# Half of the filter matrix M loaded crosswise ahead of x and copied across by GpSimd, and the filter built by channel halves ahead of x's stage

## The chip, the cores and the metric

The kernel runs on one core of one Trainium2 chip. The metric is the device time of one execution in microseconds (us), given as the median of several runs. A core has a TensorE (PE; its weight loads are shown as PEld), a VectorE (DVE), a ScalarE (ACT), a GpSimd (POOL) and a SyncE (SP); POOL and SP issue the kernel's DMAs, each in the order of its own queue.

## The reference

```python
def _attn_ref(x, h):                      # x: 8 x 5696 x 128, h: 5696 x 128
    L = 2 * S                             # S = 5696, D = 128
    Xf = np.fft.rfft(x, n=L, axis=1)
    Hf = np.fft.rfft(h, n=L, axis=0)
    y = np.fft.irfft(Xf * Hf[None], n=L, axis=1)[:, :S, :]      # a long causal convolution

def _moe_ref(x, w_r, w_i, w_ch):          # x is y of the above, n_modes = 64
    X = np.fft.rfft(x, axis=1)
    # the lowest 64 modes are mixed over channels by a complex 128 x 128 matrix each
    Yr = einsum('bmd,mde->bme', Xr, w_r) - einsum('bmd,mde->bme', Xi, w_i)
    Yi = einsum('bmd,mde->bme', Xr, w_i) + einsum('bmd,mde->bme', Xi, w_r)
    u = x + irfft(Y)
    return u + relu(u @ w_ch)
```

Inputs and output are float32; the kernel works in float16 with float32 sums in PSUM.

## The kernel before

**Tiling.** A sequence of 5696 positions is cut into NQ = 89 rows of J = 64. A transform of length 11392 is taken in two steps: a step over the 89 rows (constant `f1_sb`, NK = 90 frequencies with real and imaginary part), and then a step over the 64 positions with twiddle factors, for each frequency k by its own 64 x 192 block of the constant M (`m_sb`, line 222): the columns are minus the imaginary part, the real part, the imaginary part. Two batches are taken together ("a pair"); there are four pairs.

**The prologue**, which the change rewrites, runs in this order.

- POOL issues h's load into `h_in` (two DMAs, float32 to float16), then the first pair's x in eight pieces of two DMAs each into `x_raw` (tile Xr), then M in six pieces (lines 386-388). M is stored twice in the constant, in partitions 0-63 and again in 64-127 shifted by 64 columns, so that both halves of the partitions hold all of it.
- DVE clears half of Hp and of Xin, and ACT the rest of Xin. PE runs `idle(57, 6)`, 57 matmuls on f1 that fill the time until h lands.
- DVE copies h into Hp in four parts (line 413). The **h stage** (lines 416-429) has 16 tiles of 16 matmuls (a 128 x 64 block of Hp as weights against 90 columns of f1); each tile's result of 128 x 720 is evacuated into Ah by ACT, or by DVE for every fourth one. Behind every second tile's evacuation DVE runs `x_place` (line 359), which copies one piece of x from Xr into Xin.
- **x's stage** (lines 672-677) has 32 tiles of `a_tile` (line 444): four matmuls with 128 x 128 of Xin as weights against 180 columns of f1, evacuated into As (128 x 720), by ACT or DVE as the function `share` decides from planned costs. Every `a_tile` needs all eight pieces of x in place. Between these tiles stand twelve `filter_couple`s (line 463): eight frequencies of the filter each, one 128 x 128 matmul per frequency of M against Ah, evacuated as 128 x 1024 into Hs. When a group of couples is complete, SP moves its two partition halves crosswise within Hs (tile Hs from Hs, ten DMAs).
- `idle(4)`, and then the **main stage**: for each pair 23 ticks of `second` (M against As), `products` (times the filter Hs), `third` and `modes_of`, and then the next pair's x stage of 32 `a_tile`s. After the last pair comes the output stage.

PSUM has eight banks; the x stage takes them two at a time in the order of `SLOTS = [0, 2, 4, 6]`. Each engine runs its own list in the order in which the program adds operations; a recorder (`Recorder`, line 21) puts a semaphore wait before an operation wherever its inputs or its room depend on another engine. So DVE's list, for instance, is in program order: a copy that waits holds up the evacuations behind it.

Other places that the text below speaks of: `clear_zt` (line 511), a POOL memset; `reflect` (line 518), a DVE `tensor_scalar` from SBUF to SBUF near the output stage.

Of the kernel before, what the change touches and what calls it, by code (L numbers as in the profile page):

```python
# [123 lines left out]
def bass_long_conv_fft__then__afno_spectral_mix_kernel(nc, x, h, moe_w_r, moe_w_i, moe_w_ch, out):  # L124
# [20 lines left out]
    strip = np.stack([-mat.imag, mat.real, mat.imag], axis=2).reshape(J, NK * 3 * J)  # L145
    MW = NK * 3 * J + J
    mt = np.zeros((P, MW))
    mt[0:J, 0:NK * 3 * J] = strip
    mt[J:P, J:MW] = strip
    th = 2.0 * np.pi * np.outer(pp, pp) / J  # L150
# [55 lines left out]
    def at(name, cols, dt, off):  # L206
        return nc.alloc_sbuf_tensor_at(name, [P, cols], dt, offset=off)
# [26 lines left out]
    DH = D // 2  # L234
    hp_sb = at("Hp", J * XS, F16, a_as)
    XC = 4
    XN = J // XC
    XB = XN * D
    x_raw = [at(f"Xr{i}", XB, F16, a_h + 2 * XB * i) for i in range(2 * XC)]
    x_st = [at(f"Xt{i}", XB, F16, a_as + i * XB * 2) for i in range(2 * XC)]  # L240
# [48 lines left out]
    def pv(bank, off, dims, p0=0, n=P):  # L289
        return bass.AP(ps, p0 * 4096 + bank * 512 + off, [[4096, n]] + [list(d) for d in dims])  # L290
# [5 lines left out]
    def bank(i):  # L296
        return ("bank", i)
# [18 lines left out]
    def dma(eng, dst, src, ring, reads=(), writes=(), after=()):  # L316
        R.add(eng, lambda h_: h_.dma_start(dst, src), reads, writes, ring=ring, after=after)  # L317

    def mm(o, l, r, st, sp, reads, writes):
        R.add("tensor", lambda h_: h_.matmul(o, l, r, start=st, stop=sp), reads, writes)  # L320
# [11 lines left out]
    def turns(name, items):  # L332
        i = ring2.get(name, 0)
        ring2[name] = i + 1
        return items[i % len(items)]
# [3 lines left out]
    dma("sync", f1_sb[:, :], c_f1.ap(), "c", (), [("f1",)])  # L339
    zr = [t_[J:P, 0:J * XS].bitcast(U32) for t_ in (hp_sb, x_sb)]  # L340
    R.add("vector", lambda e: e.memset(zr[0], 0), (), [("hz",)])
# [32 lines left out]
    wp = w_pieces()  # L374
    WD = [p_[3] for p_ in wp]
    for i in range(2 * XC):
        x_load(0, i, x_raw[i], [("xr", i, 0), ("xr", i, 1)])
    XZ = [("xz", 0), ("xz", 1)]
    XIN = [("xin", i) for i in range(2 * XC)]
    XR = [[("xr", i, p_) for p_ in range(2)] for i in range(2 * XC)]  # L380
    MP = 6
    GP = 2 * KT
    NS = NK // 2 + 1
    NG = (NS + GP - 1) // GP
    KP = NK // MP
    for i in range(MP):
        lo, hi = i * KP * 3 * J, (i + 1) * KP * 3 * J + (J if i == MP - 1 else 0)
        dma("gpsimd", m_sb[:, lo:hi], bass.AP(c_m, lo, [[MW, P], [1, hi - lo]]), "x", (), [("m", i)])
    dma("sync", sg_sb[:, :], c_sg.ap(), "c", (), [("sg",)])
    dma("sync", wc_sb[:, :], bass.AP(c_w, 0, [[3 * P, P], [1, 2 * P]]), "c", (), [("wc",)])  # L390

    def mtok(k):
        t = [("m", k // KP)]
        if k % KP == KP - 1 and k < NK - 1:
            t.append(("m", k // KP + 1))
        return t

# [13 lines left out]
    DC = D // 4  # L411
    for c_ in range(4):
        R.add("vector", lambda e, c_=c_: e.tensor_copy(
            bass.AP(hp_sb, c_ * DC, [[J * XS, NQ], [XS, J], [1, DC]]),
            bass.AP(h_in, c_ * DC, [[J * D, NQ], [D, J], [1, DC]])), HT, [("hp", c_)])
    for j in range(16):
        t = turns("h", [0, 2, 4])
        for i in range(8):
            d = 8 * j + i
            for r in range(2):  # L420
                mm(pv(t + i // 4, (i % 4) * NK, [[1, NK]], J * r, J), ap(hp_sb, J * XS, 0, P, d, [[XS, J]]),
                   ap(f1_sb, 2 * NK, 0, P, r, [[2, NK]]), True, True,
                   [("hz",), ("hp", d // DC), ("f1",)], [bank(t + i // 4)])
        evac(bass.AP(ah_sb, 8 * j, [[HW, P], [D, NK], [4, 2], [1, 4]]),
             pv(t, 0, [[1, NK], [512, 2], [NK, 4]]),
             [bank(t), bank(t + 1)], [("ah", j)], 1.0 / 64,
             eng="vector" if j % 4 == 1 else "scalar")
        if j % 2 == 0:
            x_place(j // 2, x_raw[j // 2], XR[j // 2])

    load = {"scalar": 0.0, "vector": 0.0}
    COST = {720: (670, 815), 1024: (910, 1130), 256: (280, 330)}

    def share(n):
        a, v = load["scalar"] + COST[n][0], load["vector"] + COST[n][1]
        e = "scalar" if a <= v else "vector"
        load[e] = min(a, v)
        return e

    HP = [("hz",)] + [("hp", c_) for c_ in range(4)]  # L440
# [22 lines left out]
    def filter_couple(c_, sl, eng):  # L463
        ks = [k for t in (2 * c_, 2 * c_ + 1) if t < NT for k in ticks[t]]
        n = len(ks)
        for i, k in enumerate(ks):
            mm(pv(sl + i // KT, i % KT * D, [[1, D]]), m_sb[:, k * 3 * J + J:k * 3 * J + 3 * J], ah_sb[:, k * D:k * D + D], True, True,
               AHT + mtok(k) + [("ag", k)], [bank(sl + i // KT)])
        lo, t1 = ks[0] * D, min(2 * c_ + 1, NT - 1)
        hi = lo + n * D  # L470
        old = once("xr", [t_ for r_ in XR for t_ in r_]) if c_ == 0 else []
        evac(h_sb[:, lo:hi], pv(sl, 0, [[1, n * D]]), [bank(sl), bank(sl + 1)], [("h", t, 0) for t in range(2 * c_, t1 + 1)],
             eng=eng, after=old)
        if t1 in HEND:
            g0 = ([-1] + HEND)[HEND.index(t1)] + 1
            lo = KT * g0 * D
            for p0, p1 in ((0, J), (J, 0)):
                dma("sync", h_sb[p0:p0 + J, HW + lo:HW + hi], h_sb[p1:p1 + J, lo:hi], "s", [("h", i, 0) for i in range(g0, t1 + 1)],
                    [("h", i, 1, p0) for i in range(g0, t1 + 1)])
# [8 lines left out]
    def load_w(i):  # L488
# [6 lines left out]
            [("zs", i, b) for i in range(NZ) for b in range(2)]  # L495
    M_ALL = [("m", i) for i in range(MP)]
    G_ALL = [("g", i) for i in range(NG)]
    WT = [("w", i) for i in range(NWP)]
    ZY = [("zs", i, b) for i in range(NZL, NZX) for b in range(2)]
    ZX = [("zs", i, b) for i in range(NZ, NZL) for b in range(2)]  # L500
    zt_old = [(AST, AST), (AST, AST), (H_ALL, H_ALL), (H_ALL, H_ALL), (M_ALL[3:6], G_ALL)]

# [12 lines left out]
    def load_ib():  # L515
        dma("gpsimd", ib_sb[:, 0:SH], c_ib.ap(), "p", (), [("ib", 0)], after=M_ALL[0:2] + pace)

# [9 lines left out]
    def load_s4(part):  # L527
        n = PB + RB if part else P
        dma("gpsimd", s4_sb[part][0:n, 0:SH], bass.AP(c_s4, part * SH, [[2 * SH, n], [1, SH]]), "p", (),
            [("s4", part, 0)], after=pace + (AST if part else M_ALL[1:4]))  # L530

# [13 lines left out]
    def load_wi():  # L545
        dma("gpsimd", wi_sb[:, P:2 * P], bass.AP(c_w, 2 * P, [[3 * P, P], [1, P]]), "p", (), [("i16",)], after=M_ALL[5:6])
        dma("gpsimd", wi_sb[:, 0:P], moe_w_ch, "w", (), [("wch",)], after=M_ALL[5:6])

# [24 lines left out]
    def second(g_, t):  # L573
        sl = slot_of(g_, t)
        for i, k in enumerate(ticks[t]):
            for r in range(2):
                for b in range(2):
                    col = k * 3 * J + (J if r == 0 else 0) + b * J
                    mm(pv(sl + b, i * D, [[1, D]]),
                       ap(m_sb, MW, J * b, J, col, [[1, P]]),  # L580
                       ap(a_sb, AW, J * b, J, (2 * k + r) * D, [[1, D]]), r == 0, r == 1,
                       AST + mtok(k), [bank(sl + b)])

# [86 lines left out]
    NH = (NT + 1) // 2  # L670
    done = 0
    for j in range(32):
        a_tile(j, [turns("s", SLOTS)], "both" if j == 31 else share(720))
        due = NH if j == 30 else max(0, j - 3) * (NH - 1) // 26
        while done < due:
            filter_couple(done, turns("s", SLOTS), share(1024 if done + 1 < NH else 256))
            done += 1
    idle(4, turns("s", SLOTS))
# [91 lines left out]
    XTT = [(n, g_) for g_ in range(NP) for n in ("xt", "xtn")]  # L770
    reflect("vector", s4_sb[0], P, 0, ("s4", 0), M_ALL[1:4])
    reflect("scalar", s4_sb[1], PB + RB, 1, ("s4", 1), AST)
# [27 lines left out]
    for hb in range(2):  # L800
        evac(c_sb[:, hb * 512:hb * 512 + 512], ps16[:, (6 + hb) * 1024:(6 + hb) * 1024 + 512], [bank(6 + hb)],
             [("c", hb)], 2.0 * 64 / S, eng="vector" if hb else "scalar", after=WT)
    reflect("vector", ib_sb, P, 2, ("ib",), M_ALL[0:2])

# [3 lines left out]
    o8_old = [H_ALL] * 2 + [U_ALL] + [G_ALL + ZX] * 2 + [WT] * 2  # L808
    o_old = [H_ALL] * 2 + [M_ALL[5:6], U_ALL + [("f1",)]]
    NW = S // P  # L810
# [97 lines left out]
```

## Time and profile before

| | us |
|---|---|
| runs (three) | 378.55, 379.19, 380.36; median 379.19 |
| profiled execution | 379.64, of which the span from the first to the last instruction is 377.9 |
| h stage on PE | 12.95 to 28.35 |
| x's stage with the filter in it, to the first matmul of the main stage | 29.31 to 49.34 |
| busy share of the span | PE 95%, ACT 82%, DVE 80%, POOL 22% |
| granted PE clock | 0.996 |

The profile's page gives each engine's busy time, the span in 40 slices, the chain of work that ended last, and groups of equal instructions with their mean duration. The timeline gives instructions in order of time, with neighbours of one kind merged ("x8"), and the idle time before them with what ended it in brackets. Times in the timeline count from the span's start. SPq and POOLq are the issuing of DMAs; the transfers run later.

### The profile page before, as it was taken

To read this page: it belongs to the slowest core of one execution; us is meant where nothing else is said; L and a number is where in the kernel's file an instruction comes from. 1 tells how busy PE (TensorE), PEld (TensorE's weight loads), DVE (VectorE), ACT (ScalarE), POOL (GpSimd) and SP (SyncE) were. 2 spreads that over 40 slices of the span, in tenths; PEclk is the share of its full clock that TensorE was granted. 3 is DMA by queue.
4 is the path that set the end of the run, shared out by engine and by line. 5 is a ranking of instruction groups with operands and counts; after the bars stand their busy time and mean duration, and the time that the engine had idled before them with its cause. 6 is when DMAs were issued, how large, how long until landed. Compare 5 with 4: busy or idle time off the path is not lost.

```text
span 377.9 us, 11952 instructions
## 1 busy us (share of the span) xinstructions
PE 358.2 (95%) x5107; PEld 275.4 (73%) x5107; DVE 303.4 (80%) x332; ACT 311.3 (82%) x493; POOL 84.1 (22%) x137
## 2 busy tenths in 40 slices
PE   7998989999989999899999899999999999999993
PEld 4897856667856667766668666668898897888872
DVE  7567998998989998889998888767356776777784
ACT  8358989998989998999998899994467766776783
POOL 8500012220832312823203211349000000000000
PEclk9999999999999999999999999999999999999998
DMA  7999699997999996999997599999999999999977
GB/s 139 201 280 355 153 229 242 274 271 223 114 140 231 242 267 164 147 147 238 248 261 129 151 288 265 295 332 408 408 399 403 400 407 415 404 408 376 361 283 301
DMA packets 84560, 103.92 MB, mean 275 GB/s; under 512 B 22126, under 2 KB 68974, under 8 KB 81538
## 3 DMA queue, kind: packets, MB, share of 16 engines
q1 hardware_dynamic: 59643, 67.73, 51.7%
q0 software_dynamic: 24864, 35.43, 44.8%
q8 instruction: 40, 0.66, 0.7%
q14 instruction: 13, 0.11, 0.1%
HBM read 70.61 MB, written 51.12 MB: 322 GB/s over the span
## 4 chain that ended last, share of the span: by engine, by line
PE 75%; ACT 10%; DVE 7%; DMA 5%; issue 1%; SPq 0%; DVEq 0%
PE ps L320 75%; ACT As L310 7%; DMA ZT0b<-zscr 4%; DVE As L314 3%; ACT R L842 1%; DVE U L597 1%; ACT UT L308 1%; DVE Hs L312 1%; DVE UT L312 1%; DMA F<-cF 0%; DVE IBs L525 0%; ACT XT L310 0%; DVE O L843 0%; ACT Hs L308 0%; SPq L317 0%
## 5 line engine op out<-in xcount | busy, mean ns | idle before, releaser
L320 PE MATMUL ps<-U,Wc 128*128 128x512 f16 (+1 forms) x368 | 94.5, 376 | 0.0
L605 DVE TENSOR_TENSOR U<-Xs,Hs 128x2048 f16<-128x2048 f16 (+1 forms) x68 | 80.5, 1188 | 10.9 <-ACT Xs L308 8.8
L308 ACT CAST Xs<-ps 128x1024 f16<-128x1024 f32 (+1 forms) x72 | 69.5, 971 | 7.0 <-PE ps L320 4.8
L843 DVE TENSOR_TENSOR O<-ps,R 128x512 f32<-128x512 f32 x81 | 52.5, 685 | 21.4 <-ACT R L842 14.8
L308 ACT CAST Zs<-ps 128x512 f16<-128x512 f32 (+1 forms) x126 | 66.1, 605 | 0.0
L842 ACT ACTIVATE R<-ps 128x512 f32<-128x512 f32 x96 | 51.1, 573 | 14.4 <-PE ps L320 13.9
L314 DVE TENSOR_SCALAR As<-ps 128x720 f16<-128x720 f32 (+1 forms) x60 | 49.8, 878 | 8.0 <-PE ps L320 6.9
L310 ACT ACTIVATE As<-ps 128x720 f16<-128x720 f32 (+1 forms) x72 | 51.4, 772 | 5.5 <-PE ps L320 4.5
L320 PE MATMUL ps<-F,Xin 128*128 128x180 f16 x512 | 52.8, 249 | 2.8 <-ACT Ah L310 1.0
L320 PE MATMUL ps<-As,M 64*128 64x128 f16 x1440 | 48.7, 217 | 4.3 <-DVE U L597 3.5
L320 PE MATMUL ps<-WI,UT 128*128 128x256 f16 x360 | 51.9, 279 | 0.6 <-DVE O L843 0.5
L320 PEld LDWEIGHTS ps<-F,Xin 128*128 128x128 f16 x512 | 45.1, 155 | 9.7 <-DVE As L314 2.7
L320 PEld LDWEIGHTS ps<-U,Wc 128*128 128x128 f16 x368 | 28.2, 97 | 28.9 <-ACT Zs L308 6.8
L320 PEld LDWEIGHTS ps<-As,M 64*128 64x128 f16 x1440 | 40.3, 94 | 10.9 <-DVE U L597 4.2
L317 POOL DMA_DIRECT2D Xt<-in_x_dram x48 | 24.8, 520 | 100.1 <-PE ps L320 99.5
L605 DVE TENSOR_TENSOR U<-ps,Hs 128x2048 f16<-128x2048 f32 x20 | 45.7, 2284 | 0.0
L308 ACT CAST UT<-ps 128x712 f16<-128x712 f32 x40 | 30.0, 752 | 18.6 <-PE ps L320 17.8
L320 PEld LDWEIGHTS ps<-WI,UT 128*128 128x128 f16 x360 | 39.2, 152 | 4.5 <-issue 2.2
L320 PE MATMUL ps<-IBs,C 128*128 128x356 f16 x128 | 39.2, 314 | 0.9 <-DVE UT L312 0.2
L320 PEld LDWEIGHTS ps<-G,Zs 128*128 128x128 f16 x492 | 27.0, 96 | 12.7
L308 ACT CAST Zt<-ps 128x512 f16<-128x512 f32 (+1 forms) x58 | 31.0, 605 | 0.1
L320 PE MATMUL ps<-G,Zs 128*128 128x2 f16 (+2 forms) x492 | 30.3, 192 | 0.0
(88 smaller groups left out, 495.5 us busy)
## 6 DMA issues: line engine op xcount, KB each, us to landing
out_dram<-O SPq DMA_DIRECT2D x39, 512.0 KB, 12.7
zscr<-Zs SPq DMA_DIRECT2D x60, 256.0 KB, 6.5
Xt<-in_x_dram POOLq DMA_DIRECT2D x24, 320.0 KB, 6.7
zscr<-Zt SPq DMA_DIRECT2D x28, 256.0 KB, 6.5
W<-wscr POOLq DMA_DIRECT2D x8, 512.0 KB, 5.3
M<-cM POOLq DMA_DIRECT2D x5, 720.0 KB, 20.2
ZT0a<-zscr SPq DMA_DIRECT2D x3, 1024.0 KB, 14.8
Xr<-in_x_dram POOLq DMA_DIRECT2D x8, 320.0 KB, 13.6
```

The source lines that it names most:

```text
L308: R.add(e, lambda h_: h_.copy(dst, src), reads, writes, after=after)
L310: R.add(e, lambda h_: h_.activation(dst, src, COPY, scale=scale), reads, writes, after=after)
L312: R.add(e, lambda h_: h_.tensor_copy(dst, src), reads, writes, after=after)
L314: R.add(e, lambda h_: h_.tensor_scalar_mul(dst, src, scale), reads, writes, after=after)
L317: R.add(eng, lambda h_: h_.dma_start(dst, src), reads, writes, ring=ring, after=after)
L320: R.add("tensor", lambda h_: h_.matmul(o, l, r, start=st, stop=sp), reads, writes)
L597: R.add("vector", lambda e, b=b, s_=s_: e.tensor_tensor(bass.AP(u_s[i], b * 512, [[2048, P], [1024, 2], [1, n * D]]), s_, hv, MULT), [tok, ...
L605: R.add("vector", lambda e: e.tensor_tensor(uv, src, hv, MULT), bk + [("h", t, 0), ("h", t, 1, 0), ("h", t, 1, J)], [("u", i)])
L842: R.add("scalar", lambda e: e.activation(rv, src_r, RELU), bk, [("r", i % NR)], after=once(("r", i % NR), G_ALL + XTT + [("y", q) for q in ...
L843: R.add("vector", lambda e: e.tensor_tensor(ov, src_u, rv, ADD), bk + [("r", i % NR)], [key + (h_,)], after=once(key, old))
```

## The change

M is stored once. In the constant the 90 frequencies are cut into MP = 6 pieces of KP = 15; pieces 0, 2, 4 lie in partitions 0-63 and pieces 1, 3, 5 in partitions 64-127 at the same columns. Three DMAs of 128 x 2880 load this, issued by POOL between h's load and x's, where six of the same size followed x's before. Then six `tensor_copy`s on GpSimd (`m_cross`), each 64 partitions x 2880, copy every piece to the other half of the partitions, into the columns beside it. `m_col` finds a block's columns for either half; `mtok` gives the token to wait for.

The h stage handles channels d and d + 64 together: Hp holds 2 x 64 columns for each channel of a half, and 64 matmuls (16 tiles of four) take 128 x 128 of Hp against all 180 columns of f1. Ah holds the first 64 channels in partitions 0-63 and the last 64 in partitions 64-127. Evacuations are shared out by `share`. Hp's four copies are made in the order 0, 2, 1, 3; tiles 0-7 need parts 0 and 2, tiles 8-15 parts 1 and 3.

A filter couple now has 32 matmuls (real and imaginary part, and two channel halves, each with 64 partitions of M against 64 columns of Ah). All twelve couples come before x's stage, evacuated by ACT except couples 1, 5 and 9, which are DVE's. `x_place` stands between the couples, behind couples 0, 1, 3, 5, 7, 9, 10 and 11. Then come 14 idle matmuls, and then the 32 tiles of x's stage with nothing between them. SP's crosswise moves of Hs wait for the last piece of x as well. Xr moves from Hs's room to As's and the stage buffers'.

```diff
-    mt[0:J, 0:NK * 3 * J] = strip
-    mt[J:P, J:MW] = strip
+    mt = np.concatenate([np.concatenate([strip[:, i * MC:i * MC + MC], strip[:, (i + 1) * MC:(i + 2) * MC]], axis=0)
+                         for i in range(0, MP, 2)], axis=1)
...
+    HS = DH + 2
+    HPW = 2 * J * HS
+    hp_sb = at("Hp", HPW, F16, a_as)
...
+    for i in range(0, MP, 2):
+        dma("gpsimd", m_sb[:, i * MC:i * MC + MC], bass.AP(c_m, i // 2 * MC, [[MP // 2 * MC, P], [1, MC]]), "x", (),
+            [("m", 0, i), ("m", 1, i + 1)])
     for i in range(2 * XC):
         x_load(0, i, x_raw[i], [("xr", i, 0), ("xr", i, 1)])
+
+    def m_cross(i, eng):
+        up, lo, o_ = m_sb[0:J, :], m_sb[J:P, :], i // 2 * 2 * MC
+        (d_, s_), (k_, v_) = (((lo, up), (("m", 1, i), ("m", 0, i))) if i % 2 == 0 else ((up, lo), (("m", 0, i), ("m", 1, i))))
+        R.add(eng, lambda e: e.tensor_copy(d_[:, o_ + MC:o_ + 2 * MC], s_[:, o_:o_ + MC]), [v_], [k_])
+
+    def m_col(c, k, r):
+        return ((k // KP) ^ c) * MC + k % KP * 3 * J + (J if r == 0 else 0)
...
-    for i in range(MP):
-        lo, hi = i * KP * 3 * J, (i + 1) * KP * 3 * J + (J if i == MP - 1 else 0)
-        dma("gpsimd", m_sb[:, lo:hi], bass.AP(c_m, lo, [[MW, P], [1, hi - lo]]), "x", (), [("m", i)])
...
-    for j in range(16):
-        t = turns("h", [0, 2, 4])
-        for i in range(8):
-            d = 8 * j + i
-            for r in range(2):
-                mm(pv(t + i // 4, (i % 4) * NK, [[1, NK]], J * r, J), ap(hp_sb, J * XS, 0, P, d, [[XS, J]]),
-                   ap(f1_sb, 2 * NK, 0, P, r, [[2, NK]]), True, True,
-                   [("hz",), ("hp", d // DC), ("f1",)], [bank(t + i // 4)])
...
-        if j % 2 == 0:
-            x_place(j // 2, x_raw[j // 2], XR[j // 2])
...
+    for c_ in (0, 2, 1, 3):
+        dst = bass.AP(hp_sb, c_ // 2 * J * HS + c_ % 2 * DC, [[HPW, NQ], [HS, J], [1, DC]])
+        src = bass.AP(h_in, c_ * DC, [[J * D, NQ], [D, J], [1, DC]])
+        R.add("vector", lambda e, dst=dst, src=src: e.tensor_copy(dst, src), HT, [("hp", c_)])
+    for i in range(MP):
+        m_cross(i, "gpsimd")
+    H2 = D // 2
+    load["vector"] = 600.0
+    for j in range(16):
+        t = turns("h", [0, 2, 4, 6])
+        for i in range(4):
+            d = 4 * j + i
+            mm(pv(t + i // 2, (i % 2) * 2 * NK, [[1, 2 * NK]]), ap(hp_sb, HPW, 0, P, d, [[HS, 2 * J]]), f1_sb[:, :], True, True,
+               [("hz",), ("hp", d // DC), ("hp", (d + H2) // DC), ("f1",)], [bank(t + i // 2)])
+        evac(bass.AP(ah_sb, 4 * j, [[HW, P], [H2, 2 * NK], [2, 2], [1, 2]]),
+             pv(t, 0, [[1, 2 * NK], [512, 2], [2 * NK, 2]]),
+             [bank(t), bank(t + 1)], [("ah", j)], 1.0 / 64, eng=share(720))
...
         for i, k in enumerate(ks):
-            mm(pv(sl + i // KT, i % KT * D, [[1, D]]), m_sb[:, k * 3 * J + J:k * 3 * J + 3 * J], ah_sb[:, k * D:k * D + D], True, True,
-               AHT + mtok(k) + [("ag", k)], [bank(sl + i // KT)])
+            for r in range(2):
+                for c in range(2):
+                    mm(pv(sl + c, i * H2, [[1, H2]]), ap(m_sb, MW, J * c, J, m_col(c, k, r), [[1, P]]),
+                       ap(ah_sb, HW, J * c, J, (2 * k + r) * H2, [[1, H2]]), r == 0, r == 1,
+                       AHT + mtok(k, c) + [("ag", k)], [bank(sl + c)])
...
-                dma("sync", h_sb[p0:p0 + J, HW + lo:HW + hi], h_sb[p1:p1 + J, lo:hi], "s", [("h", i, 0) for i in range(g0, t1 + 1)],
+                dma("sync", h_sb[p0:p0 + J, HW + lo:HW + hi], h_sb[p1:p1 + J, lo:hi], "s", XR[-1] + [("h", i, 0) for i in range(g0, t1 + 1)],
...
-    done = 0
+    x_at = [0, 1, 3, 5, 7, 9, 10, 11]
+    for c_ in range(NH):
+        filter_couple(c_, turns("s", SLOTS), "vector" if c_ % 4 == 1 else "scalar")
+        for i in range(2 * XC):
+            if x_at[i] == c_:
+                x_place(i, x_raw[i], XR[i])
+    idle(14, turns("s", SLOTS))
+    load.update(scalar=0.0, vector=0.0)
     for j in range(32):
         a_tile(j, [turns("s", SLOTS)], "both" if j == 31 else share(720))
-        due = NH if j == 30 else max(0, j - 3) * (NH - 1) // 26
-        while done < due:
-            filter_couple(done, turns("s", SLOTS), share(1024 if done + 1 < NH else 256))
-            done += 1
```

What is left out here only renames the tokens of M's pieces in later waits, and lets `second` take its columns from `m_col`; its matmuls keep their shapes and number.

More of the change, by code (lines that the diff above doesn't have):

```diff
@@ L145, in bass_long_conv_fft__then__afno_spectral_mix_kernel @@
     strip = np.stack([-mat.imag, mat.real, mat.imag], axis=2).reshape(J, NK * 3 * J)
-    MW = NK * 3 * J + J
-    mt = np.zeros((P, MW))
-    mt[0:J, 0:NK * 3 * J] = strip
-    mt[J:P, J:MW] = strip
+    MP = 6
+    KP = NK // MP
+    MW = NK * 3 * J
+    MC = KP * 3 * J
+    mt = np.concatenate([np.concatenate([strip[:, i * MC:i * MC + MC], strip[:, (i + 1) * MC:(i + 2) * MC]], axis=0)
+                         for i in range(0, MP, 2)], axis=1)
     th = 2.0 * np.pi * np.outer(pp, pp) / J
@@ L234, in bass_long_conv_fft__then__afno_spectral_mix_kernel @@
     DH = D // 2
-    hp_sb = at("Hp", J * XS, F16, a_as)
+    HS = DH + 2
+    HPW = 2 * J * HS
+    hp_sb = at("Hp", HPW, F16, a_as)
     XC = 4
@@ L238, in bass_long_conv_fft__then__afno_spectral_mix_kernel @@
     XB = XN * D
-    x_raw = [at(f"Xr{i}", XB, F16, a_h + 2 * XB * i) for i in range(2 * XC)]
+    x_raw = [at(f"Xr{i}", XB, F16, a_as + 2 * HPW + 2 * XB * i if i < 5 else a_st + 2 * J * D + 2 * XB * (i - 5)) for i in range(2 * XC)]
+    assert HPW + 5 * XB <= AW and J * D + 3 * XB <= (2 * NU + NXS + NZ) * 1024
     x_st = [at(f"Xt{i}", XB, F16, a_as + i * XB * 2) for i in range(2 * XC)]
@@ L339, in bass_long_conv_fft__then__afno_spectral_mix_kernel @@
     dma("sync", f1_sb[:, :], c_f1.ap(), "c", (), [("f1",)])
-    zr = [t_[J:P, 0:J * XS].bitcast(U32) for t_ in (hp_sb, x_sb)]
+    zr = [hp_sb[J:P, :].bitcast(U32), x_sb[J:P, 0:J * XS].bitcast(U32)]
     R.add("vector", lambda e: e.memset(zr[0], 0), (), [("hz",)])
@@ L380, in bass_long_conv_fft__then__afno_spectral_mix_kernel @@
     XR = [[("xr", i, p_) for p_ in range(2)] for i in range(2 * XC)]
-    MP = 6
     GP = 2 * KT
@@ L384, in bass_long_conv_fft__then__afno_spectral_mix_kernel, with mtok @@
     NG = (NS + GP - 1) // GP
-    KP = NK // MP
-    for i in range(MP):
-        lo, hi = i * KP * 3 * J, (i + 1) * KP * 3 * J + (J if i == MP - 1 else 0)
-        dma("gpsimd", m_sb[:, lo:hi], bass.AP(c_m, lo, [[MW, P], [1, hi - lo]]), "x", (), [("m", i)])
     dma("sync", sg_sb[:, :], c_sg.ap(), "c", (), [("sg",)])
     dma("sync", wc_sb[:, :], bass.AP(c_w, 0, [[3 * P, P], [1, 2 * P]]), "c", (), [("wc",)])
[L392 to L396, printed above, removed]
+    def mtok(k, c):
+        return [("m", c, k // KP)]
     W1, W2, WI = wc_sb[:, 0:P], wc_sb[:, P:2 * P], wi_sb[:, :]
@@ L411, in bass_long_conv_fft__then__afno_spectral_mix_kernel @@
     DC = D // 4
[L412 to L415, printed above, removed]
-    for j in range(16):
-        t = turns("h", [0, 2, 4])
-        for i in range(8):
-            d = 8 * j + i
-            for r in range(2):
-                mm(pv(t + i // 4, (i % 4) * NK, [[1, NK]], J * r, J), ap(hp_sb, J * XS, 0, P, d, [[XS, J]]),
-                   ap(f1_sb, 2 * NK, 0, P, r, [[2, NK]]), True, True,
-                   [("hz",), ("hp", d // DC), ("f1",)], [bank(t + i // 4)])
[L424 to L427, printed above, removed]
-        if j % 2 == 0:
-            x_place(j // 2, x_raw[j // 2], XR[j // 2])
     load = {"scalar": 0.0, "vector": 0.0}
@@ L466, in filter_couple @@
         for i, k in enumerate(ks):
-            mm(pv(sl + i // KT, i % KT * D, [[1, D]]), m_sb[:, k * 3 * J + J:k * 3 * J + 3 * J], ah_sb[:, k * D:k * D + D], True, True,
-               AHT + mtok(k) + [("ag", k)], [bank(sl + i // KT)])
+            for r in range(2):
[3 more added lines that the diff above has]
+                       AHT + mtok(k, c) + [("ag", k)], [bank(sl + c)])
         lo, t1 = ks[0] * D, min(2 * c_ + 1, NT - 1)
         hi = lo + n * D
-        old = once("xr", [t_ for r_ in XR for t_ in r_]) if c_ == 0 else []
-        evac(h_sb[:, lo:hi], pv(sl, 0, [[1, n * D]]), [bank(sl), bank(sl + 1)], [("h", t, 0) for t in range(2 * c_, t1 + 1)],
-             eng=eng, after=old)
+        evac(bass.AP(h_sb, lo, [[2 * HW, P], [H2, 2], [D, n], [1, H2]]), pv(sl, 0, [[512, 2], [H2, n], [1, H2]]), [bank(sl), bank(sl + 1)],
+             [("h", t, 0) for t in range(2 * c_, t1 + 1)], eng=eng)
         if t1 in HEND:
@@ L495, in bass_long_conv_fft__then__afno_spectral_mix_kernel @@
             [("zs", i, b) for i in range(NZ) for b in range(2)]
-    M_ALL = [("m", i) for i in range(MP)]
+    MS = [[("m", 0, i), ("m", 1, i ^ 1)] for i in range(MP)]
+    M_ALL = [t_ for m_ in MS for t_ in m_]
     G_ALL = [("g", i) for i in range(NG)]
@@ L500, in bass_long_conv_fft__then__afno_spectral_mix_kernel @@
     ZX = [("zs", i, b) for i in range(NZ, NZL) for b in range(2)]
-    zt_old = [(AST, AST), (AST, AST), (H_ALL, H_ALL), (H_ALL, H_ALL), (M_ALL[3:6], G_ALL)]
+    zt_old = [(AST, AST), (AST, AST), (H_ALL, H_ALL), (H_ALL, H_ALL), (M_ALL[6:12], G_ALL)]
     def load_zt(i, eng="sync", more=()):
@@ L515, in load_ib @@
     def load_ib():
-        dma("gpsimd", ib_sb[:, 0:SH], c_ib.ap(), "p", (), [("ib", 0)], after=M_ALL[0:2] + pace)
+        dma("gpsimd", ib_sb[:, 0:SH], c_ib.ap(), "p", (), [("ib", 0)], after=M_ALL[0:4] + pace)
     def reflect(eng, t, n, col, key, after):
@@ L529, in load_s4 @@
         dma("gpsimd", s4_sb[part][0:n, 0:SH], bass.AP(c_s4, part * SH, [[2 * SH, n], [1, SH]]), "p", (),
-            [("s4", part, 0)], after=pace + (AST if part else M_ALL[1:4]))
+            [("s4", part, 0)], after=pace + (AST if part else M_ALL[2:8]))
     V, A = "vector", "scalar"
@@ L545, in load_wi @@
     def load_wi():
-        dma("gpsimd", wi_sb[:, P:2 * P], bass.AP(c_w, 2 * P, [[3 * P, P], [1, P]]), "p", (), [("i16",)], after=M_ALL[5:6])
-        dma("gpsimd", wi_sb[:, 0:P], moe_w_ch, "w", (), [("wch",)], after=M_ALL[5:6])
+        dma("gpsimd", wi_sb[:, P:2 * P], bass.AP(c_w, 2 * P, [[3 * P, P], [1, P]]), "p", (), [("i16",)], after=M_ALL[10:12])
+        dma("gpsimd", wi_sb[:, 0:P], moe_w_ch, "w", (), [("wch",)], after=M_ALL[10:12])
     LC, LM = 2, 3
@@ L577, in second @@
                 for b in range(2):
-                    col = k * 3 * J + (J if r == 0 else 0) + b * J
                     mm(pv(sl + b, i * D, [[1, D]]),
-                       ap(m_sb, MW, J * b, J, col, [[1, P]]),
+                       ap(m_sb, MW, J * b, J, m_col(b, k, r), [[1, P]]),
                        ap(a_sb, AW, J * b, J, (2 * k + r) * D, [[1, D]]), r == 0, r == 1,
-                       AST + mtok(k), [bank(sl + b)])
+                       AST + mtok(k, b), [bank(sl + b)])
     def products(g_, t, sl):
@@ L770, in bass_long_conv_fft__then__afno_spectral_mix_kernel @@
     XTT = [(n, g_) for g_ in range(NP) for n in ("xt", "xtn")]
-    reflect("vector", s4_sb[0], P, 0, ("s4", 0), M_ALL[1:4])
+    reflect("vector", s4_sb[0], P, 0, ("s4", 0), M_ALL[2:8])
     reflect("scalar", s4_sb[1], PB + RB, 1, ("s4", 1), AST)
@@ L802, in bass_long_conv_fft__then__afno_spectral_mix_kernel @@
              [("c", hb)], 2.0 * 64 / S, eng="vector" if hb else "scalar", after=WT)
-    reflect("vector", ib_sb, P, 2, ("ib",), M_ALL[0:2])
+    reflect("vector", ib_sb, P, 2, ("ib",), M_ALL[0:4])
     n_o = [0]
@@ L808, in bass_long_conv_fft__then__afno_spectral_mix_kernel @@
     o8_old = [H_ALL] * 2 + [U_ALL] + [G_ALL + ZX] * 2 + [WT] * 2
-    o_old = [H_ALL] * 2 + [M_ALL[5:6], U_ALL + [("f1",)]]
+    o_old = [H_ALL] * 2 + [M_ALL[10:12], U_ALL + [("f1",)]]
     NW = S // P
```

## The prediction

> **What bounds the kernel now.** The change rewrites the first 50 us; afterwards the same matmuls run. So I read the chain of waits up to there first.
>
> ```profile
> 2.53 25.84 PE ps L320 x313
> 28.39 0.78 ACT Ah L310
> 29.31 0.84 PE ps L320 x8
> 30.17 2.54 DVE As L314 x3
> 32.71 1.14 DVE Hs L312
> ...
> 48.57 1.44 PE ps L320 x20
> 50.01 1.22 DVE U L597
> ```
>
> No DMA but f1's stands in it. To 28.37 it is PE (warm-up, then the h stage); from 29.31 it passes between PE and the evacuations, of As and Hs alike. The table of windows (PE, PEld, DVE, ACT, POOL busy) says what is full in each stage:
>
> ```profile
> 5.00:10.00 5.00, 5.00 (x32) 3.05 (x31) 3.73 (x2) 4.64 (x1) 5.00 (x11) 1.00 0.91 193
> 12.95:28.35 15.40, 15.40 (x257) 15.28 (x256) 10.10 (x15) 8.47 (x11) 1.52 (x3) 1.00 1.06 253
> 33.90:48.60 14.70, 14.00 (x167) 12.09 (x168) 14.02 (x15) 14.09 (x20) 0.00 (x0) 1.00 0.70 187
> ```
>
> The h stage is PE: 256 small matmuls at 15.40/256 = 60 ns, evacuators half idle. In x's stage DVE and ACT are 95% full. The first row prices an idle matmul: 5.00/32 = 0.156 us.
>
> The third view is the timeline of DVE and of POOL where the two engines meet, far from the change, but the only place with POOL work of this kind:
>
> ```profile
> 254.54 3.60 DVE L525 TENSOR_SCALAR S4a<-S4a,SG 128x2759 f16<-128x2759 f16 x1
> 260.59 0.42 DVE L314 TENSOR_SCALAR C<-ps 128x512 f16<-128x512 f16 x1 [0.82 <-PE ps L796]
> 260.93 1.45 DVE L525 TENSOR_SCALAR IBs<-IBs,SG 128x2759 f16<-128x2759 f16 x1
> ```
>
> POOL's, of the same timeline:
>
> ```profile
> 253.83 1.82 POOL L513 MEMSET ZT1b<- 32x2048 uint32 x1
> 255.57 1.82 POOL L513 MEMSET ZT2b<- 32x2048 uint32 x1
> ...
> 259.80 1.84 POOL L513 MEMSET ZT3b<- 32x2048 uint32 x1
> ```
>
> Two equal SBUF-to-SBUF operations on DVE take 3.60 and 1.45 us. IBs ends 0.74 us behind the memset of ZT3b (261.64 to 262.38); S4a ends 0.75 us behind the **second** of two memsets that run back to back (257.39 to 258.14). So 0.75 us is its work, and the rest is standing still while POOL holds something; between the two memsets DVE did not get in. The operation on C reads PSUM, runs in the middle of a memset and takes 0.42 us: that kind does not wait.
>
> **The change without any stall.** The end to move is 49.34, where the first matmul of the main stage starts.
>
> *Loads.* h lands about 11.75, as now (DVE starts on it at 11.83). The waits of x's placing are on DMA and spaced 3.73 us per two pieces, so a piece of x takes 1.87 us and the first lands at 13.5. M's 720 KB pieces, at the 426 GB/s that the DMA row shows behind x, take 1.73 us: they land at 13.5, 15.2 and 17.0, and the last x at 17.0 + 8 x 1.87 = 31.9, placed (0.68) at 32.6. On POOL's queue x's issues come 3 x 0.65 later, which the transfers hide; the crossing copies stand behind the last x issue, at about 12.5. The three loads of M that are gone hid nothing: no one waited for M.
>
> *h stage.* 64 matmuls in a_tile's shape: 28 of those took 2.68 us, so 6.1 us in all. Evacuation binds: following `share`, ACT has 9 tiles at 0.72 (15 in 10.77 in a later pass), DVE 7 at 0.85 (2.54 for three) behind Hp's four copies, which end at 14.35. Both end near 20.5, where the stage now ends at 29.2.
>
> *Couples.* 32 matmuls of 64 x 128 weights: `second` has that shape, and its weight loads take 0.90 us for 32 (with twice the columns behind them, 1.07: the upper bound). Eleven couples and a quarter: 10.1 us, 12.0 at most. ACT's eight evacuations at 1.01 and DVE's three at 1.22 with eight placings at 0.68 fit beside that. PE ends at 30.6; 14 idle matmuls make it 32.8, just behind x.
>
> *x's stage* alone: 27 tiles of a later pass take 10.77 us, so 32 take 12.8, and 0.5 to fill: 13.3. End 46.1, that is **-3.2 us**. SP's moves of Hs now start at 31.9; ten DMAs of 2.9 MB at 220 GB/s (35 to 40 us gave 231) are through at 45, before the main stage; later groups are needed ticks later. If that cover is gone, only tick 0's small group counts.
>
> **The copies on GpSimd.** The trace shows no POOL copy. Nearest row: the memset, 2048 elements in 1.82 us, 0.89 ns each; 2880 elements then cost 2.56 us. Were it bytes that count, 5760 against 8192 give 1.28; were reading and writing two passes, 5.1. I take 2.56. Six make 15.4 us. Piece p is first needed by couples 0, 1, 3, 5, 7, 9; the last one is due at 20.5 + 9 x 0.9 = 28.6, and they end at 13.6 + 15.4 = 29.0. By themselves they almost fit.
>
> But DVE's copies of h and its placings of x are SBUF to SBUF at 0.33 ns per element, the kind of S4a, and the six crossings follow each other with all their data there. By the S4a row the first placing, due at 20.6, stands until the crossings end. Whether Hp's fourth copy stands too is a race: it starts at 13.66, and M's first piece lands at 13.5, with the wait and the start of a POOL instruction to come. I take it that DVE wins; the crossings then run from 14.35 to E = 14.35 + 15.4 = 29.7.
>
> Behind the first placing are queued couple 1's evacuation and all that follows on DVE. Couple 5 needs couple 1's banks, so PE stops at 25.0, after couple 4. DVE places (0.75) and evacuates (1.2): PE resumes at E + 1.95 = 31.7. Couples 5 to 11 take 6 x 0.9 + 0.25 = 5.65 (couples 5 and 9, evacuated by DVE between placings, just keep up), the idle ones 2.2: x's stage starts at 39.5 and ends at 52.8. That is **+3.5 us** against 49.34. The profiled execution took 379.64, 1.74 around its span of 377.9, and the median of three is 379.19, 0.45 less; put on the median, 382.7.
>
> **Rivals.**
>
> *POOL wins the race.* Hp's fourth copy stands from 13.66 to E = 13.6 + 15.4 = 29.0, with DVE's seven h tiles behind it; PE stops around tile 6. Then the copy 0.7, seven evacuations 6.0, couples 10.1, idle 2.2, x's stage 13.3: 61.3, +12.0, **391.2**. For it: M's 13.5 before 13.66. Against: the start of a POOL copy.
>
> *DVE gets in between two crossings.* [...] In numbers: the first placing waits for the third crossing (22.0), then couple 1 to 23.9, the next placings behind one crossing each, to 26.0 and 29.2, couple 5 to 30.4; the crossings end late, at 31.8, and couple 9 starts there. Three couples and the idle ones: 36.1, end 49.4, no change, **379.3**.
>
> *The cover holds* and the change does what it says: -3.2, **376.0**. It needs crossings by bytes (1.28 us: they end at 22.0, and the placing loses only 1.4 us, inside the slack of four bank pairs), or a POOL copy that does not stop DVE. The point that decides: E + 23.1 = 49.34, so E = 26.2 and 1.98 us per crossing. For it: the value lies between 1.28 and 2.56, and the S4a row is of memsets, not copies.
>
> *Two passes, 5.1 us each:* E = 45.0, end 68.1, **398**. [...]
>
> **How the numbers follow.** Forecast (placings stand, Hp's copy does not) 0.34; POOL wins 0.18; DVE in between 0.14; cover holds 0.26; two passes 0.08. A measurement of this kernel tells about 0.5%, 1.9 us, from no change. Faster: the cover, and 0.02 of "in between" where it comes out cheaper, 0.28. Same: the rest of "in between", 0.12. Slower: the others, 0.60. The range reaches from 375.4 (the cover's 376.0, less the 0.64 by which the lowest run shown lies under the median) to 391.8 (POOL's 391.2 and as much); 398 is left out. Forecast's own range, for couples at 12.0 us and crossings of 2.3 to 3.0: 381 to 387.
>
> **What would show it.** In the profile after: six POOL copies, near 2.56 us from start to start, from about 14.4; the first placing of x on DVE with a duration of some 9 us instead of 0.68, ending 0.7 behind the last crossing; PE idle before couple 5; x's stage (32 tiles) 13.3 us long; the first `second` at 52.8. A fourth copy of Hp of 15 us means POOL won. Placings of 0.7 to 3 us each mean that DVE gets in. Placings of 0.7 throughout with PE busy from 13 to 46 us mean that I was wrong about the meeting of the two engines, or about the copy's price; crossings of over 3 us with PE waiting on POOL at couples 1 to 9 mean that the price was too low.

## The result, and the profile after

The changed kernel takes 383.44 us (median of four, 382.81 to 384.20) against 379.57 for the kernel before; the ratio is 1.0101 with a 95% interval of 1.0076 to 1.0127. The forecast was 382.7 and slower. The profiled execution took 383.11 with a span of 381.3, so 3.4 us more span than before.

The sign and the size were forecast, but only part of the way to them. In the chain of waits (start, duration, what) two places account for the 3.4 us:

```profile
12.04 4.89 DVE Hp L433 x4
16.93 0.83 DVE Ah L319
...
28.13 3.06 DVE Xin L365
31.20 1.14 DVE Hs L317
32.38 16.89 PE ps L325 x202
51.36 1.22 DVE U L607
...
259.50 2.34 issue
261.84 1.66 PE ps L325 x47
```

First, x's stage now starts behind a placing of x on DVE that took 3.06 us, and the main stage starts at 50.70 instead of 49.34: **+1.36 us**, where +3.5 was forecast. Second, PE stops for **2.34 us** at 259.5 in the middle of a run of equal matmuls, at the start of the output stage, where the change did nothing. PE's timeline shows the row of 64 in which it falls, first in the kernel before, then in the changed one:

```profile
257.27 2.03 PE L320 MATMUL ps<-XT,W 128*128 128x64 f16 x64
```
```profile
258.61 0.89 PE L325 MATMUL ps<-XT,W 128*128 128x64 f16 x25
261.84 1.32 PE L325 MATMUL ps<-XT,W 128*128 128x64 f16 x39 [2.34 <-issue]
```

The difference between the kernels grows there from 1.33 (254.88 against 253.55) to 3.87 us (263.73 against 259.86), and some of it comes back later.

DVE's timeline of the prologue, and POOL's:

```profile
12.04 4.89 DVE L433 COPY Hp<-Hin 89x2048 f16<-89x2048 f16 x4 [2.42 <-DMA Hin<-in_h_dram]
16.85 6.01 DVE L319 TENSOR_SCALAR Ah<-ps 128x720 f16<-128x720 f32 x7
22.77 2.44 DVE L365 COPY Xin<-Xr 89x2048 f16<-89x2048 f16 x1
25.14 1.21 DVE L317 CAST Hs<-ps 128x1024 f16<-128x1024 f32 x1
26.27 4.92 DVE L365 COPY Xin<-Xr 89x2048 f16<-89x2048 f16 x2
31.12 1.21 DVE L317 CAST Hs<-ps 128x1024 f16<-128x1024 f32 x1
32.25 1.28 DVE L365 COPY Xin<-Xr 89x2048 f16<-89x2048 f16 x2
```
```profile
13.73 16.92 POOL L390 COPY M<-M 64x2880 f16<-64x2880 f16 x6 [1.53 <-DMA M<-cM]
```

The six copies on GpSimd take 16.92 us, 2.82 each. While they run, Hp's four copies take 4.89 instead of 2.52 and three placings of x 7.36 instead of 2.05. The evacuations from PSUM between them (0.89 each in the h stage, 1.21 each in the couples) take what they took in the kernel before (0.91 and 1.22). The moment the copies are over, two placings take 1.28 together.

PE's timeline of the couples shows a second such stop, which the prediction did not have either:

```profile
22.91 2.51 PE L325 MATMUL ps<-Ah,M 64*128 64x64 f16 x160 [1.00 <-DVE Ah L319]
26.40 1.20 PE L325 MATMUL ps<-Ah,M 64*128 64x64 f16 x70 [0.98 <-DVE Hs L317]
30.03 1.73 PE L325 MATMUL ps<-Ah,M 64*128 64x64 f16 x58 [2.43 <-issue]
32.38 2.10 PE L325 MATMUL ps<-Ah,M 64*128 64x64 f16 x72 [0.62 <-DVE Hs L317]
34.41 2.97 PE L325 MATMUL ps<-F 128*128 128x360 f16 x14
```

160 matmuls in 2.51 us are 15.7 ns each, 0.50 us a couple. Then PE stops for 2.43 us with nothing to wait for ("issue"), inside couple 7, behind 57 + 64 + 160 + 70 = 351 matmuls from the start. In this changed kernel the stop is not on the path to the main stage: behind it PE still waits 0.62 us for DVE. In the same slices PE's granted clock falls (the third number from the end):

```profile
25.00:30.00 5.00, 1.62 (x100) 1.38 (x92) 5.00 (x4) 3.39 (x4) 4.94 (x2) 0.90 0.97 191
30.00:35.00 5.00, 4.35 (x133) 3.81 (x134) 5.00 (x6) 2.61 (x3) 0.65 (x1) 0.50 0.56 120
```

So there were two questions: how long DVE stands behind a copy on GpSimd, and what stops PE.

### The profile page after: what moved, and what is told of

The parts are those of the page before. It is cut to its first block, busy times and chain, and to the rows that moved or that the text cites. A ratio compares the mean times of both kernels' runs of the same rounds, so it can differ in the third digit from the quotient of the medians.

```text
span 381.3 us, 12139 instructions
## 1 busy us (share of the span) xinstructions
PE 354.6 (93%) x5199; PEld 270.3 (71%) x5199; DVE 310.9 (82%) x333; ACT 310.7 (81%) x492; POOL 98.1 (26%) x140
## 4 chain that ended last, share of the span: by engine, by line
PE 76%; ACT 9%; DVE 8%; DMA 3%; issue 2%; DVEq 0%; POOL 0%; POOLq 0%
PE ps L325 76%; ACT As L315 7%; DMA Hin<-in_h_dram 3%; DVE As L319 2%; DVE Xin L365 1%; DVE U L607 1%; DVE Hp L433 1%; ACT R L855 1%; ACT UT L313 1%; DVE Hs L317 1%; DVE Ah L319 0%; DVE IBs L536 0%; DVE UT L317 0%; ACT XT L315 0%; DVE O L856 0%
## 5 line engine op out<-in xcount | busy, mean ns | idle before, releaser
L319 DVE TENSOR_SCALAR As<-ps 128x720 f16<-128x720 f32 (+1 forms) x63 | 51.9, 878 | 7.1 <-PE ps L325 5.8
L315 ACT ACTIVATE As<-ps 128x720 f16<-128x720 f32 (+1 forms) x69 | 49.1, 775 | 6.4 <-PE ps L325 5.7
L325 PE MATMUL ps<-F,Xin 128*128 128x180 f16 x512 | 51.9, 249 | 1.5 <-DVE As L319 0.8
```

The source lines that it names most:

```text
L315: R.add(e, lambda h_: h_.activation(dst, src, COPY, scale=scale), reads, writes, after=after)
L319: R.add(e, lambda h_: h_.tensor_scalar_mul(dst, src, scale), reads, writes, after=after)
```

## The experiments

The times below are medians on one chip for each group; the kernel before had 379.87 us beside the first four runs and 380.10 beside the last four.

### What stops PE: the stream moved by some matmuls

The two theories were that PE's stops are loads of its code, tied to a place in the instruction stream, or that they follow from the changed work. The changed kernel's page counts 41 packets of the instruction queue, 0.67 MB, for 5199 matmuls and as many weight loads; if all of them are PE's, that is an estimate of 254 of PE's instructions for each packet. Two kernels have other matmuls in the warm-up and nothing else.

```diff
-    idle(WARM, 6)
+    tiny(44, 6)          # 16 weight and 16 moving columns each; in the kernel before: 114
+    idle(WARM - 8, 6)    # in the kernel before: WARM - 22
```

The changed kernel, moved by 36 matmuls:

> The changed kernel with 8 of the 57 warm-up matmuls replaced by 44 tiny ones (16 columns), which moves everything behind them by 36 matmuls in PE's instruction stream and takes about the same time. Theory 'position': PE's pause of 2.34 us near 259.5 us is a load of code that falls into a dense stretch of matmuls, and depends only on where the stream is cut into blocks of some 256 instructions; moved by 36 matmuls the cut lies where the kernel before has it, the pause goes, and the time is 2.4 us lower, about 381.0; the main stage starts near 50.7 as in the changed kernel, give or take 1 us if the cut inside the couples (2.43 us near 27.6) moves as well. Rival 'consequence': the pause follows from the changed work itself (loads that come later, another order of transfers); it stays, and the time is 383.4.

380.62 us, 1.0024 (1.0001 to 1.0047) of the kernel before, so 2.9 us less than the change had (the two intervals do not overlap), although the main stage starts at 51.41 here, 0.7 later. The stop at the start of the output stage is gone: the 64 matmuls in which it fell run through in one row. And in the couples PE stops again, at another place of the filter, but behind the same number of matmuls of the stream: 44 + 49 + 64 + 194 = 351. PE's timeline, first at the start of the output stage, then in the couples:

```profile
259.30 2.03 PE L325 MATMUL ps<-XT,W 128*128 128x64 f16 x64
```
```profile
24.27 3.10 PE L325 MATMUL ps<-Ah,M 64*128 64x64 f16 x194 [1.10 <-DVE Ah L319]
30.58 4.92 PE L325 MATMUL ps<-Ah,M 64*128 64x64 f16 x166 [3.21 <-issue]
```

The kernel before, moved by 92 matmuls, as the change moves it:

> The kernel before with 22 of the 57 warm-up matmuls replaced by 114 tiny ones, which puts everything behind them 92 matmuls later in the stream, as the changed kernel has it from x's stage on. 'Position': the pause appears near 258 us though none of the change is in, and the time is some 2.4 us higher, about 381.9. 'Consequence': no pause, 379.5.

382.81 us, 1.0088 (1.0057 to 1.0119). A kernel with no part of the change in it loses nearly as much as the change did. The stop appears inside the same row of 64, though with 0.90 us, in PE's timeline:

```profile
260.36 0.86 PE L320 MATMUL ps<-XT,W 128*128 128x64 f16 x24
262.13 1.33 PE L320 MATMUL ps<-XT,W 128*128 128x64 f16 x40 [0.90 <-issue]
```

The rest of its loss lies elsewhere: its main stage starts at 50.91 instead of 49.34, with a granted clock of 0.69 at the start of x's stage, and PE waits 1.05 us for a load of G at 57. So of the 3 us, the stop itself is one. Whether the others follow from the moved stream or from the other warm-up is open: the granted clock is down to 0.60 already at 15 to 20 us, in the h stage, where the kernel before had 1.00. The clock alone does not make the loss, since an execution of this kernel with a mean clock of 0.998 took 382.80 us.

What follows: the stops are tied to the stream. In the five kernels that have the changed kernel's stream, the late one falls behind the 3672nd matmul, in the moved kernel before behind the 3671st; in the three changed kernels whose stream is moved, it is not there. Within 27.4 to 30.1 us the changed kernel's DMA rows have one packet of the instruction queue:

```profile
q0 software_dynamic: 153, 0.44, 83.6%
q8 instruction: 1, 0.02, 2.3%
```

It starts at 27.60, 0.2 us behind the start of the last matmul ahead of the stop, and takes 0.97; PE goes on 1.5 us behind its end. At the late stop the packet starts at 259.41 and takes 0.90, and PE goes on at 261.84, again 1.5 us behind its end. It is so in the traces of all nine kernels that have such stops: each of their 14 stops at these two places ends 1.3 to 1.5 us behind the end of a packet of the instruction queue. There the length of the stop goes by when the packet starts: 0.59 us where it starts 1.7 us ahead of the last matmul, 3.2 where it starts 1.2 behind. By the estimate of 254 instructions for each packet, 127 matmuls with their weight loads make up one; at 15.7 ns each they last 2.0 us. Whether the loads of x, which keep the DMA engines 83.6% busy in that window, are what makes the packet late was not tried.

### How long DVE stands: copies of half the elements

```diff
-        R.add(eng, lambda e: e.tensor_copy(d_[:, o_ + MC:o_ + 2 * MC], s_[:, o_:o_ + MC]), [v_], [k_])
+        R.add(eng, lambda e: e.tensor_copy(d_[:, o_ + MC:o_ + 2 * MC].bitcast(U32), s_[:, o_:o_ + MC].bitcast(U32)), [v_], [k_])
```

> The changed kernel with GpSimd's six copies made as uint32, 1440 elements of 4 bytes instead of 2880 of 2. Theory 'per element': 1.41 us from start to start instead of 2.82, the last one ends near 22.3 instead of 30.65; Hp's fourth copy stands for 1 us instead of 2.4, the placings of x behind the couples take 0.7 each, PE does not wait for DVE within the couples; the last x lands at 32, the main stage starts at 46.5 to 47.5 instead of 50.7, and the time is 3 to 4 us lower, 379.5 to 380.5 (the late pause stays in it). Rival 'per byte': 2.82 us each and 383.4 as now. [...]

382.14 us, 1.0056 (1.0024 to 1.0087): 0.45% below the change, less than expected, and with overlapping intervals not shown by this run alone. The copies take 1.53 each, against 2.82 for as many bytes in twice the elements: for these copies elements count, not bytes. POOL's timeline, and PE's in the couples:

```profile
13.38 9.16 POOL L390 COPY M<-M 64x1440 uint32<-64x1440 uint32 x6 [0.81 <-DMA M<-cM]
```
```profile
24.27 1.20 PE L325 MATMUL ps<-Ah,M 64*128 64x64 f16 x70 [0.31 <-DVE Hs L317]
28.68 3.34 PE L325 MATMUL ps<-Ah,M 64*128 64x64 f16 x128 [3.21 <-issue]
```

Hp's copies take 3.70, only the first placing stands (1.77), and DVE then waits for PE, not PE for DVE. But the stop behind matmul 351 is still there and is now on the path: the main stage starts at 48.16, 2.5 us earlier, where 46.5 to 47.5 was expected. The profiled execution was the lowest of twelve (378.54, with a late stop of only 0.59 us); they reach to 383.78, so the 2.5 us need not hold for all of them.

### The copies on DVE

```diff
-    for i in range(MP):
-        m_cross(i, "gpsimd")
...
+        if j in (2, 4, 6, 8, 10, 12):
+            m_cross(j // 2 - 1, "vector")
+            load["vector"] += 850.0
```

> The changed kernel with the six copies on DVE instead of GpSimd, one behind each of the h tiles 2, 4, 6, 8, 10 and 12, counted with 850 in the sharing out of evacuations. Theory 'standing': a copy costs DVE 0.8 to 0.9 us, and nothing stands any more; the h stage ends near 22.5, the couples near 30, x's stage starts when the last x is placed, at 33, and the main stage near 46.5: time 4 us lower, about 379.5 with the late pause in it. Rival 'DVE is short': the copies put 5 us on DVE in the h stage and its end moves to 25 or later; then main stage near 48.5 and 381.5.

382.59 us, 1.0065 (1.0031 to 1.0099). Nothing on DVE stands any more (Hp 2.50, every placing 0.7), and a copy costs DVE 0.9. But `share` now gives ACT 13 of the 16 h tiles, and ACT ends them at 22.8, so the couples start at 22.98 as in the changed kernel, and PE's stop comes behind, in the chain of waits:

```profile
14.10 8.74 ACT Ah L315 x13
22.84 0.14 issue
22.98 5.08 PE ps L325 x230
28.05 2.71 issue
30.77 3.45 PE ps L325 x128
```

The main stage starts at 50.26. The h stage ends near the 22.5 that was expected, and not at 25 as the rival had it; the 46.5 for the main stage and the 379.5 were missed, because without the standings PE's stop bounds.

### One copy at a time, or the whole row

The forecast had DVE standing until the last of the six copies ends ("the whole row"). The changed kernel's profile already speaks against it, since the four copies on DVE that stood in it ended at 16.93, 25.22, 28.21 and 31.20, each 0.55 us behind the end of one copy on GpSimd (16.38, 24.67, 27.66 and 30.65), while the row of six went on. Two kernels test it: each copy cut into halves of 64 x 1440 (two `tensor_copy`s), and the first copy held back until Hp's fourth one is done (`after=[("hp", 3)]`). If DVE gets in behind each single copy ("one at a time"), the halves should halve every standing, with the main stage 0.5 to 1.5 us earlier than 50.7 and a time of about 382.5; if the copies hold DVE off together, the standings should stay as long as with six, at 383.4.

> The changed kernel with each of GpSimd's six copies cut into two of 64 x 1440: twelve copies of some 1.45 us, the same 17 us in all. [...]

383.33 us, 1.0094 (1.0059 to 1.0129). The standings halve as "one at a time" has it: Hp's copies 3.69, the first placing 1.51, the next four 2.53 for each pair. The time does not follow, against the expectation: DVE now gets in more often and holds up the copies in turn (1.73 to 1.85 instead of 1.40 where it does), the last one ends at 32.8 instead of 30.65, and couples wait for M, so that the main stage starts at 52.34, 1.6 later than in the changed kernel, where 0.5 to 1.5 earlier was expected. PE's timeline:

```profile
26.20 0.90 PE L325 MATMUL ps<-Ah,M 64*128 64x64 f16 x50 [1.44 <-POOL M L392]
28.70 0.50 PE L325 MATMUL ps<-Ah,M 64*128 64x64 f16 x11 [1.60 <-issue]
29.77 1.78 PE L325 MATMUL ps<-Ah,M 64*128 64x64 f16 x59 [0.58 <-POOL M L392]
32.90 1.78 PE L325 MATMUL ps<-Ah,M 64*128 64x64 f16 x60 [1.35 <-POOL M L392]
```

> The changed kernel with GpSimd's first copy waiting for Hp's fourth one. Theory: Hp's copies take 2.5 us instead of 4.9, the h stage ends at 20.5 to 21.5 instead of 22.9; the copies on GpSimd end 0.7 later, the placings stand one copy each as now, PE's pause in the couples stays; the main stage starts 0.3 to 1.2 earlier, the time is 382.3 to 383.2. Rival (the forecast's 'whole row'): with nothing to let it in, the first placing stands until the last copy ends at 31, and the main stage starts at 52 or later.

382.96 us, 1.0085 (1.0056 to 1.0115), with the main stage at 50.08, 0.6 earlier, both as expected: the race that POOL won cost 0.6 in the profiled executions, too little for the times to show. The first placing stands for one copy although all six follow each other from 15.00, in DVE's timeline:

```profile
15.11 6.15 DVE L319 TENSOR_SCALAR Ah<-ps 128x720 f16<-128x720 f32 x7 [0.18 <-PE ps L325]
21.18 2.24 DVE L365 COPY Xin<-Xr 89x2048 f16<-89x2048 f16 x1
23.34 1.20 DVE L317 CAST Hs<-ps 128x1024 f16<-128x1024 f32 x1
```

"The whole row" is refuted for these copies. One copy and DVE's own 0.68 make at most 2.82 + 0.68 = 3.50 us: the placing took 2.24 here, and the longest one in the changed kernel 3.06; in none of these traces did one stand for two. What a copy on GpSimd holds meanwhile no trace shows.

### Both causes taken away

uint32 copies with the stream moved by 36:

> The changed kernel with the copies as uint32 and the stream moved by 36 matmuls. Theory: both gains add up: no pause near 257, main stage near 48.2 as with uint32 alone (25.5 to 28.7 PE still stops before its 351st matmul, since that place in the stream is fixed): 378.3 to 379.3, 0.2 to 0.4% below the kernel before. Rival: where the cut falls in the couples decides more; main stage later than 49, and 380 or more.

379.07 us, 0.9987 (0.9953 to 1.0021): level with the kernel before, and within the 378.3 to 379.3 that was expected. In the times the two gains add up: moving the stream takes 0.77% off with the copies as they were (1.0101 to 1.0024) and 0.69% with uint32 copies (1.0056 to 0.9987); uint32 copies take off 0.45% without the move and 0.37% with it. Each uint32 step alone lies within overlapping intervals; that it comes out twice speaks for it. In the profiled execution they do not add up: the late stop is gone, but x came later (the last placing ended at 35.85 and bounded x's stage, main stage at 49.46).

Then the version that the runs point to. It has the uint32 copies, and a stream moved by 54 small matmuls for 8 of the warm-up; with ten idle matmuls fewer ahead of x's stage, all behind them stands where moving by 36 put it. What is new beside these:

```diff
-    x_at = [0, 1, 3, 5, 7, 9, 10, 11]
+    x_at = [0, 1, 3, 5, 7, 8, 8, 11]
...
-    idle(14, turns("s", SLOTS))
+    idle(4, turns("s", SLOTS))
```

> uint32 copies, two placings of x moved ahead of couple 9's evacuation (x_at 0, 1, 3, 5, 7, 8, 8, 11), 4 idle matmuls instead of 14 ahead of x's stage, and 46 + 8 tiny matmuls for 8 of the warm-up, so that the later stream stands as in the kernel before. Theory: x's stage starts when the last x is placed, 33.3, instead of 34.7; the main stage starts at 46.8, no late pause: 377 to 378, 0.5 to 0.7% below the kernel before. Rival: without the idle matmuls PE's clock is half when x's stage starts, which costs 0.5 to 1 us of it; or the pause in the couples ends behind 33; then 378.5 to 379.5.

378.08 us, **0.9950** (0.9915 to 0.9985) of the kernel before, 1.5% below the change as it was made; 377 to 378 was expected. The main stage starts at 47.10. PE still stops behind matmul 351 (103 + 64 + 160 + 24), now 3.07 us, but early, where x is still on its way, in PE's timeline:

```profile
20.78 2.51 PE L325 MATMUL ps<-Ah,M 64*128 64x64 f16 x160 [1.00 <-DVE Ah L319]
23.47 0.52 PE L325 MATMUL ps<-Ah,M 64*128 64x64 f16 x24 [0.18 <-DVE Hs L317]
27.06 3.23 PE L325 MATMUL ps<-Ah,M 64*128 64x64 f16 x128 [3.07 <-issue]
31.34 0.87 PE L325 MATMUL ps<-Ah,M 64*128 64x64 f16 x48 [1.04 <-issue]
32.14 0.78 PE L325 MATMUL ps<-F 128*128 128x360 f16 x4
33.55 12.61 PE L325 MATMUL ps<-F,Xin 128*128 128x180 f16 x128 [0.62 <-DVE Xin L365]
```

x's stage starts at 33.55, when the last x is placed, and takes what it took with 14 idle matmuls ahead of it (12.61 against 12.54). The rival that it would start on half the clock is refuted: the granted clock from 33.55 to 36.00 is 1.00. The second stop, of 1.04 us, falls 128 matmuls behind the first, after the 479th, so 128 matmuls and 128 weight loads further on, about the 254 instructions of a packet; the kernel with the copies on DVE and the two others with uint32 copies have one of 0.28 to 0.41 us there.

## Why the prediction was right, and where it was not

**The direction's cause held, for the prologue.** SBUF-to-SBUF copies on DVE stood while GpSimd copied (placings of x up to 3.06 us instead of 0.68), PSUM evacuations did not (1.21 against 1.22), and this turns a forecast gain of 3.2 us in the prologue into a loss. Taking half of the copies' time away brings 2.5 us back (48.16 against 50.70) in the profiled execution, and 0.4% in the times. The path was the forecast one too: PE stops behind couple 4, after 160 matmuls, and waits for DVE to free the banks of couple 1.

**The size came out by luck, by two errors that cancel.** The prologue lost 1.36 us, not 3.5. The other 2 us are PE's stop at 259.5, which no step of the prediction had; the runs with a moved stream put it at some 0.7% of the time, the larger part of the loss. A reader who had only the total would take the mechanism for confirmed in full.

By its steps:

- *Whole row or one copy.* The step read S4a's 3.60 us behind two memsets as a rule for copies. It failed: DVE got in behind the one copy that ran, each time, and the wait of PE for couple 1 was 0.98 us where 6.7 (25.0 to 31.7) was forecast. No view of the kernel before shows a placing that waits for one copy alone, as that rival's numbers take it; in the profile after, the first three placings ended 0.55 us behind the end of one copy each. The profile shows the prediction's own sign for "DVE gets in between", placings of 0.7 to 3 us (0.68 to 3.06), and that rival's +0.1 us in the prologue was nearer to the measured +1.36 than the forecast was. S4a stands behind both memsets in the changed kernel again (3.60 us). One difference can be read off: the second memset starts 0.08 us before the first one ends (255.57 against 255.65), while the copies leave 0.05 to 0.06 us between them, as far as POOL's records go. Whether that is why memsets hold on and copies do not was not tried.
- *The race.* "I take it that DVE wins" failed: the first copy started at 13.73 and Hp's fourth one stood 2.4 us. Since it stood for one copy only, it cost 0.6 in the profiled executions, not the 12 of that rival.
- *The copy's price.* 2.56 from the memset's 0.89 ns per element; measured 2.82, or 0.98 ns, on average; from start to start 2.64 where DVE did not get in and 2.99 where it did. Elements count in these copies (1.53 us for half as many of twice the size), so the bound by bytes (1.28) and that by two passes (5.1) both fall.
- *Couples.* 0.90 us each from `second`'s weight loads; measured 0.50 for matmuls and weight loads alike (160 weight loads in 2.39 us, 0.48 for 32). The matmuls have half as many columns as those of `second`; why the weight loads are so much shorter was not tried. It made room that PE's stop took back.
- *Loads, h stage, x's stage.* The first piece of M at 13.5 (the copy on it starts at 13.73) and the last x at 31.9 (the first of SP's moves of Hs, which wait for it, starts at 32.01) were within 0.3. x's stage from its first matmul to the main stage was 13.48 against 13.3. The h stage without a standing ended at 21.3 (with Hp's copies first) against 20.5.
- *The idle matmuls* took 2.8 instead of 2.2 us; behind PE's stop the granted clock was 0.50 (30 to 35 us).

The last experiment shows how much of the cover could be had: -2.2 us in the prologue against the kernel before, in the profiled execution, where the sum without stalls said -3.2.

## What to carry to other kernels

Before work goes to GpSimd, list what DVE copies from SBUF to SBUF at that time and what is queued behind it: here such a copy, 0.68 us by itself, took up to 3.06 beside copies of 2.82 on GpSimd. So make those short in elements (the bitcast of 2-byte to 4-byte elements brought them here from 2.82 to 1.53 us) and put the placings where nothing urgent follows. A change of PE's instruction count can show far away from the change: here 92 matmuls more in the prologue came with a stop of 2.34 us at 259.5, and 36 more took it away. Before a difference of under 1% is put down to a change, look for stops without a releaser inside rows of equal matmuls, and move the stream by some harmless instructions to see whether they stay.

## What the runs showed of the hardware that was not expected

- PE stopped for 2.4 to 3.2 us behind its 351st matmul in all of the changed kernel's variants in which M was there in time, and for 1.6 and 2.1 us in the two where it had waited for M shortly before; wherever the stream was moved to, the number stayed. In the changed kernel the packets of the instruction queue around it start at 21.30, 27.60 and 31.17, 6.3 and 3.6 us apart, where 128 matmuls of 15.7 ns last 2.0 us; that the stage ran faster than its code came is the author's reading of these times.
- The same kernel before, with only its warm-up made of more and smaller matmuls, is 0.88% slower (0.57 to 1.19); a stop of 0.90 us is one part of it, the rest is open.
- Matmuls with 64 x 128 weights and 64 columns, alternating between the two halves of the partitions, took 15.7 ns each, with 128 columns 33 ns (32 in 1.07).
